# Two chained feed-forward networks in fp32 on one core: the operands of the next pair of blocks formed over six steps with their sums kept in DRAM, the tail's weights loaded two steps ahead, the last results turned on TensorE

## The chip, the cores and the metric

The kernel runs on one core of a Trainium2 chip. The metric is the device time of one execution in microseconds (us). The engines of the core are named as the profile names them: PE (TensorE, matmul; PEld is its weight load), DVE (VectorE), ACT (ScalarE), POOL (GpSimd) and SP (SyncE, which here only issues DMAs; SPq is its queue of instructions). Each engine works through its own list in order and waits at an instruction until what that instruction needs is there.

## The reference

`x` is (8, 8, 512, 64), `state` is (8, 8, 32, 64), everything is fp32. Attention between each head's tokens and its 32 states gives 4608 rows of width 512 (512 token rows and 32 state rows of 8 batches, 8·544 = 4352 output rows in all); two feed-forward networks follow. Cut to what matters here:

```python
def _moe_ref(x, w_gate, w_val, w_out):          # d_ff = 1536
    g = x @ w_gate
    silu = g * (1.0 / (1.0 + np.exp(-g)))
    return silu * (x @ w_val) @ w_out

def _moe2_ref(x, w_in, w_out, alpha):           # d_ff = 2048, the part that is changed
    h = x @ w_in
    g = np.maximum(h, 0.0) + alpha * np.minimum(h, 0.0)
    return g @ w_out
```

## The kernel before

Every fp32 matrix product is made from three products of a high and a low part (`PASSES`, L19): an operand is split into `hi`, a rounded copy written by ACT (L77, `acopy`), and `lo`, the rest, a subtraction on DVE (L83, `sub_lo`). Attention and the first network take the first 741 us; their output goes to DRAM in `x2d`, one tile for each block of 512 tokens. The change is in the second network, which has 8 such blocks in four pairs, and then the state rows.

**A pair and its steps.** The second network works on a pair of blocks with a scheme that needs 7 products where a 2x2x2 multiplication needs 8. For it the input of a pair is wanted in seven *forms* of 128x1024 (`FORMS`: b00, t2, t1, t3, b10, t4, b11), each with hi and lo. Three of them are input blocks; four (t1 to t4) are differences, t1 = b01 − b00, t2 = b11 − t1, t3 = b11 − b01, t4 = b10 − t2. A pair has 8 *steps* s = 0..7, each for 256 of the 2048 hidden columns, so 32 steps t in all; 8 steps for the states follow (the tail, `hidden_last`, L1006 to L1022, `held`, L991).

**A step.** `hidden_pair` (L841) makes 7 products, one for each form, in the order of `FORMS`; a product is a *group* of 6 matmuls of 128x512 (L851) into the PSUM tiles g, v or aux. DVE adds parts together (`plus`, L859), ACT and POOL apply the second network's activation (`raised`, L817 to L823), POOL forms differences (`less`, L863), and the results are split into `h`. After each of the products comes a *place*: `fill()` (L1059) is called, places 1 to 7 of a step. It takes one item from `work`: a *link*, which is the multiplication with `w_out` (`project`, L944), again a group of 6 matmuls (L954) into `acc`, after which DVE adds `acc` into a tile `sum` (L965). Two steps (a *group of steps*) have 7 links for each of two halves e, 14 items; `work` starts with 16 empty items, which sets by how many places the links run behind the products. A step is therefore 14 groups of 6 matmuls on PE.

**Forming the next pair.** At s = 6 `x2_pair` puts 12 actions into the list `nxt`: four loads of raw input tiles x2r from DRAM, four subtractions of 128x1024 (L786), and seven `put`s (L771), each a hi on ACT and right behind it the lo on DVE. `FORMING` (L1048) says at which places one is taken: (s=6, places 1 and 7), all seven of s = 7, and places 1, 2 and 4 of the next pair's s = 0.

**Giving the results.** When a result tile of a pair is complete, it is queued in `giving`. `give` (L969) adds on DVE (L982), turns the 128x512 tile in 32x32 blocks on DVE (L986) and writes it with four DMAs of 64 KB in rows of 128 bytes (L989). One is taken at each third place, when `nxt` is empty; in the tail, at each place. There are eight to a pair.

**Order.** For the 32 pair steps DVE, ACT and POOL run in the order in which the code is written. The lists of PE and SP are set by a scheduler. SP issues all DMAs from one list: the weights `w2` of the products (L758), the weights `wo2` of the links (L941; `load_wo`, three links' at a group's start, then each three links ahead), x2r (L783), the weights of the tail (`load_last`, L762, one step ahead) and the output (L989). When the first of these waits for its data, all behind it wait.

## Time and profile before

| | |
|---|---|
| time, median of 3 runs | 1501.37 us (1499.89 to 1504.82) |
| the profiled execution | 1497.59 us, span 1495.7 us |
| busy: PE / DVE / ACT / POOL | 92% / 70% / 55% / 37% of the span |
| second network, 32 pair steps | 741.4 to 1401.1 us |
| tail (states, last links and results) | 1401.1 to 1495.7 us |
| mean granted PE clock | 0.977 |
| HBM traffic | 195.04 MB read, 58.20 MB written |

The busy shares are averages over two networks with different limits, so the prediction goes by stretches. A step in which PE never waits takes 19.04 us (14 groups of 6 matmuls, 1.36 us each); what a step takes above that is a wait, or slow matmuls after one. In the rows below a timeline row gives start, duration, engine, line, operation, tiles, how many, and in brackets how long the engine stood idle before it and what ended that. A row of grouped instructions ends in busy time, mean ns of one, and idle time before them.

### The profile page before, as it was taken

The numbers are of one execution on the slowest core, as the hardware profiler recorded it, in microseconds if no ns is written. First come the engines' busy times: TensorE is split into PE (matmuls) and PEld (weight loads), VectorE is DVE, ScalarE is ACT, GpSimd is POOL, SyncE is SP. The second block draws the span as 40 slices with busy tenths as digits, with TensorE's granted clock in tenths as the row PEclk, the third lists the DMA queues.
The fourth block names the chain that finished last, engine by engine and source line by source line (L and its number), as shares of the span: only waits on it lengthen the run. The fifth ranks groups of instructions, "written<-read, shape, count | busy, mean of one in ns | idle before, by whom it ended". The sixth has DMA issues, their size and how long they took to land.

```text
span 1495.7 us, 20408 instructions
## 1 busy us (share of the span) xinstructions
PE 1383.1 (92%) x7160; PEld 1066.4 (71%) x7160; DVE 1046.4 (70%) x1599; ACT 819.0 (55%) x1400; POOL 552.4 (37%) x422
## 2 busy tenths in 40 slices
PE   5799999999998999999979988999799998999895
PEld 2466777767676767779958866778577876788784
DVE  6778536677786876345556787887887788778740
ACT  6665344555655545334367655666466655666532
POOL 4432102233231331000065545655454654556511
PEclk7999999999999999999999999999999999999998
DMA  9443150776859565103255656685557756676585
GB/s 265 165 148 63 58 142 2 219 222 195 225 171 271 163 187 140 44 1 127 64 214 174 196 161 185 167 262 183 169 133 226 266 163 190 179 244 222 180 238 183
DMA packets 282142, 254.60 MB, mean 170 GB/s; under 512 B 149944, under 2 KB 210360, under 8 KB 281016
## 3 DMA queue, kind: packets, MB, share of 16 engines
q1 hardware_dynamic: 279896, 252.90, 56.1%
q8 instruction: 57, 0.93, 0.2%
q10 hardware_dynamic: 2144, 0.39, 0.2%
q14 instruction: 45, 0.37, 0.1%
HBM read 195.04 MB, written 58.20 MB: 169 GB/s over the span
## 4 chain that ended last, share of the span: by engine, by line
PE 60%; DVE 17%; ACT 8%; issue 6%; DMA 5%; POOL 2%; SPq 2%; POOLq 0%; DVEq 0%; ACTq 0%
PE acc L502 15%; PE acc L954 11%; PE v L471 9%; PE g L471 8%; PE v L851 5%; DVE h L83 5%; PE g L851 3%; PE aux L851 3%; PE aux L441 3%; DVE u L859 2%; DVE x L83 2%; DVE sum L965 2%; DMA raw<-in_moe_w_out_dram 2%; ACT m L822 1%; ACT m L820 1%
## 5 line engine op out<-in xcount | busy, mean ns | idle before, releaser
L954 PE MATMUL acc<-h,wo 128*128 128x512 f32 x1344 | 352.4, 399 | 28.0 <-DVE sum L965 18.3
L954 PEld LDWEIGHTS acc<-h,wo 128*128 128x128 f32 x1344 | 255.8, 192 | 92.7 <-DVE sum L965 24.9
L502 PE MATMUL acc<-h,wp 128*128 128x512 f32 (+1 forms) x1296 | 296.7, 379 | 7.1 <-DVE h L83 3.7
L502 PEld LDWEIGHTS acc<-h,wp 128*128 128x128 f32 x1296 | 234.0, 189 | 57.6 <-DVE h L83 4.9
L823 POOL TENSOR_TENSOR u<-u,m 128x512 f32<-128x512 f32 x96 | 125.4, 1306 | 363.4 <-ACT m L822 329.8
L83 DVE TENSOR_TENSOR h<-u,h 128x512 fp32r<-128x512 f32 x160 | 155.6, 988 | 59.7 <-ACT h L77 58.9
L851 PE MATMUL v<-x,w 128*128 128x512 f32 x576 | 151.6, 400 | 19.5 <-DVE u L859 19.5
L471 PE MATMUL g<-a,sw 128*128 128x512 f32 x576 | 155.9, 406 | 9.7 <-ACT sw L77 5.4
L471 PEld LDWEIGHTS g<-a,sw 128*128 128x128 f32 x576 | 105.1, 190 | 71.3 <-issue 26.0
L471 PE MATMUL v<-a,sw 128*128 128x512 f32 x576 | 154.4, 404 | 0.2 <-DVE p L487 0.2
L820 ACT ACTIVATE m<-u 128x512 f32<-128x512 f32 x96 | 60.4, 629 | 154.8 <-DVE u L859 154.7
L851 PEld LDWEIGHTS v<-x,w 128*128 128x128 f32 x576 | 108.9, 191 | 47.4 <-DVE u L859 25.0
L965 DVE TENSOR_TENSOR sum<-acc,sum 128x512 f32<-128x512 f32 x184 | 125.2, 682 | 20.3 <-PE acc L954 19.6
L471 PEld LDWEIGHTS v<-a,sw 128*128 128x128 f32 x576 | 107.5, 192 | 34.0 <-issue 10.1
L83 DVE TENSOR_TENSOR h<-h,h 128x512 fp32r<-128x512 f32 (+1 forms) x80 | 81.7, 1021 | 55.4 <-ACT h L77 54.8
L283 POOL TENSOR_TENSOR m<-m,raw 128x512 int32<-128x512 int32 x44 | 61.1, 1393 | 154.0 <-DVE m L275 92.1
L487 DVE TENSOR_TENSOR s<-s,v 128x512 f32<-128x512 f32 (+1 forms) x84 | 54.2, 645 | 83.0 <-PE v L471 68.4
L863 POOL TENSOR_TENSOR u<-u,u 128x512 f32<-128x512 f32 x64 | 106.1, 1658 | 5.0
L77 ACT ACTIVATE h<-u 128x512 fp32r<-128x512 f32 x160 | 96.4, 621 | 18.5 <-POOL u L863 18.5
L83 DVE TENSOR_TENSOR sw<-aux,sw 128x512 fp32r<-128x512 f32 x96 | 62.7, 683 | 56.0 <-ACT sw L77 56.0
L851 PE MATMUL aux<-x,w 128*128 128x512 f32 x384 | 98.9, 391 | 3.0 <-DVE x L83 2.3
L851 PE MATMUL g<-x,w 128*128 128x512 f32 x384 | 98.9, 393 | 2.1 <-ACT h L821 2.1
(143 smaller groups left out, 2091.1 us busy)
## 6 DMA issues: line engine op xcount, KB each, us to landing
wo<-ws2d SPq DMA_DIRECT2D x224, 256.0 KB, 3.9
w<-w2d SPq DMA_DIRECT2D x104, 512.0 KB, 5.2
w2d<-sp SPq DMA_DIRECT2D x32, 512.0 KB, 3.6
raw<-in_moe_w_out_dram SPq DMA_DIRECT2D x14, 1024.0 KB, 5.2
w<-w2d SPq DMA_DIRECT2D x48, 256.0 KB, 4.3
x2d<-xo SPq DMA_DIRECT2D x32, 256.0 KB, 3.5
raw<-in_moe_w_in_dram SPq DMA_DIRECT2D x8, 1024.0 KB, 6.3
wo2d<-sp SPq DMA_DIRECT2D x16, 512.0 KB, 4.1
```

The source lines that it names most:

```text
L77: return nc.scalar.activation(o, i, AF.Copy)
L83: (eng or nc.vector).tensor_tensor(out=o, in0=src, in1=hi.bitcast(F32), op=ALU.subtract)
L283: nc.gpsimd.tensor_tensor(out=m, in0=m, in1=lo, op=ALU.add)
L471: nc.tensor.matmul(o[:, :self.n], self.lhs(f, k, a, which), self.rhs(k, c), start=(i == 0), stop=(i == last))
L487: return nc.vector.tensor_tensor(out=self.p[f], in0=self.p[f], in1=self.product(f, 1, "v"), op=ALU.mult)
L502: nc.tensor.matmul(self.acc[e][:, :self.n], wo1[f // 2][:, f % 2, a, e * P:(e + 1) * P], t[:, c, :self.n], start=(f == 0 and i == 0), stop ...
L820: nc.scalar.activation(n, src, AF.Relu, scale=-1.0)
L823: nc.gpsimd.tensor_tensor(out=out, in0=out, in1=n, op=ALU.add)
L851: nc.tensor.matmul(o, w[:, a, q], x[k][:, q, e], start=start and n == 0, stop=stop and n == 5, skip_group_check=True)
L863: nc.gpsimd.tensor_tensor(out=o, in0=x0, in1=x1, op=ALU.subtract)
L954: nc.tensor.matmul(o, w[:, f, a, e], h[:, q], start=first and i == 0, stop=i == 5, skip_group_check=True)
L965: nc.vector.tensor_tensor(out=r, in0=o, in1=r, op=ALU.add)
```

## The change

- **Sums ahead of time, by way of DRAM.** For pairs 1 to 3 `x2_pair` gives way to two functions. `x2_sums`, registered at s = 1, loads raw tiles at (s=4, place 1), (4, 5) and (5, 4) and makes the four differences at (4, 4), (5, 1), (5, 3) and (5, 7); each is written by SP to `xt2d` in DRAM (512 KB). `x2_forms`, registered at s = 6, loads each form's source again, from `x2d` or `xt2d`, up to five places ahead, makes the hi on ACT at places 4 and 6 of s = 6, 2, 4 and 6 of s = 7, and 1 and 3 of the next s = 0, and the lo on DVE one place later. A transition has 11 loads of 512 KB in place of 4, and 4 writes more.
- **Links one place earlier.** `work` starts with 15 empty items in place of 16.
- **Gives.** The condition for taking one in a pair step is now place number divisible by three and not one of the first four places of s = 0.
- **Last pair's results.** `give_last` makes only the DVE addition; at the next place `turn` makes four PE transposes of 128x128 (L1056 of the new file) into an aux PSUM tile, ACT copies it (no DVE transpose), and one DMA in rows of 512 bytes writes it. In the tail every place takes two items of `work`.
- **Tail weights** are loaded two steps ahead.

```diff
--- before.py
+++ after.py
@@ -94,6 +94,7 @@
     x2d = [dram.tile([P, NPAIR, S if c < B else NS], F32, tag=f"x2d{c}", name=f"x2d{c}")
            for c in range(B + 1)]
     srd = dram.tile([NS, DM], F32, tag="srd", name="srd")
+    xt2d = [dram.tile([P, 4, 2, S], F32, tag=f"xt2d{c}", name=f"xt2d{c}") for c in range(1, B // 2)]
     w2d = [dram.tile([P, 8, 2, 2, P], F32, tag=f"w2d{j}", name=f"w2d{j}") for j in range(NJ2)]
     ws2d = [dram.tile([P, 7, 2, 2, P], F32, tag=f"ws2d{j}", name=f"ws2d{j}") for j in range(NJ2)]
     wo2d = [dram.tile([P, 2, 2, DM], F32, tag=f"wo2d{j}", name=f"wo2d{j}") for j in range(NJ2)]
@@ -774,6 +775,57 @@
             sub_lo(t[:, :, 1, :n], src[:, :, :n], t[:, :, 0, :n])
             return t
 
+        def x2_raw(pr, d, c):
+            t = t4([P, 2, S], F32, "x2r")
+            nc.sync.dma_start(t, x2d[2 * pr + c][:, 2 * d:2 * d + 2, :])
+            return t
+
+        def x2_sums(pr):
+
+            r = {}
+
+            def load(d, c):
+                r[d, c] = x2_raw(pr, d, c)
+
+            def sub(k, x0, x1, to):
+                nc.vector.tensor_tensor(out=r[to], in0=r[x0], in1=r[x1], op=ALU.subtract)
+                nc.sync.dma_start(xt2d[pr - 1][:, k], r[to])
+
+            b00, b01, b10, b11 = [(d, c) for d in range(2) for c in range(2)]
+            return {(4, 1): lambda: (load(*b00), load(*b01)), (4, 4): lambda: sub(0, b01, b00, b00),
+                    (4, 5): lambda: load(*b11), (5, 1): lambda: sub(2, b11, b01, b01),
+                    (5, 3): lambda: sub(1, b11, b00, b11), (5, 4): lambda: load(*b10),
+                    (5, 7): lambda: sub(3, b10, b11, b10)}
+
+        def x2_forms(pr):
+
+
+            x, places = x2.setdefault(pr, {}), {}
+
+            def load(k):
+                if FORMS[k][0] == "b":
+                    x["raw", k] = x2_raw(pr, int(FORMS[k][1]), int(FORMS[k][2]))
+                else:
+                    t = x["raw", k] = t4([P, 2, S], F32, "x2r")
+                    nc.sync.dma_start(t, xt2d[pr - 1][:, int(FORMS[k][1]) - 1])
+
+            def hi(k):
+                x[FORMS[k]] = t8([P, 2, 2, S], F32R, "x2")
+                acopy(x[FORMS[k]][:, :, 0], x["raw", k])
+
+            def lo(k):
+                t = x[FORMS[k]]
+                sub_lo(t[:, :, 1], x.pop(("raw", k)), t[:, :, 0])
+
+            def put(at, th):
+                places.setdefault((NJ2 - 2 + (at - 1) // 7 if at < 15 else 0, (at - 1) % 7 + 1), []).append(th)
+
+            for k, at in enumerate((4, 6, 9, 11, 13, 15, 17)):
+                put(max(1, at - 5), lambda k=k: load(k))
+                put(at, lambda k=k: hi(k))
+                put(at + 1, lambda k=k: lo(k))
+            return places
+
         def x2_pair(pr):
 
             r, x = {}, x2.setdefault(pr, {})
@@ -923,7 +975,7 @@
             for k, o in (("t1", h00), ("t3", h01), ("t2", h11), ("t4", h10)):
                 left[k] = lambda k=k, o=o: (hi(k, o), lo(k, o))
 
-        acc, sums, put_in, giving = {}, {}, set(), []
+        acc, sums, put_in, giving, turning = {}, {}, set(), [], []
 
         def store(u, o):
             nq = P // Ns
@@ -964,7 +1016,10 @@
             else:
                 nc.vector.tensor_tensor(out=r, in0=o, in1=r, op=ALU.add)
             if s == NJ2 - 2 and k in ("h10", "t2", "t3", "t4"):
-                giving.append(lambda: give(pr, to, e))
+                if pr < B // 2 - 1:
+                    giving.append(lambda: give(pr, to, e))
+                else:
+                    give_last(pr, to, e)
 
         def give(pr, to, e):
 
@@ -987,6 +1042,23 @@
             for i in range(4):
                 dst = out[c * T:c * T + S, d * P + 32 * i:d * P + 32 * i + 32]
                 nc.sync.dma_start(dst.rearrange("(t r) n -> r t n", r=32), o[32 * i:32 * i + 32])
+
+        def give_last(pr, to, e):
+
+            d, c = 2 * e + int(to[1]), 2 * pr + int(to[2])
+            r = sums[pr, to][:, e]
+            if to != "o00":
+                nc.vector.tensor_tensor(out=r, in0=sums[pr, "p1"][:, e], in1=r, op=ALU.add)
+
+            def turn():
+                pt = aux([P, SC, P])
+                for k in range(SC):
+                    nc.tensor.transpose(pt[:, k, :], r[:, k * P:(k + 1) * P], ident)
+                o = t2([P, SC, P], F32, "o")
+                acopy(o, pt)
+                nc.sync.dma_start(out[c * T:c * T + S, d * P:(d + 1) * P].rearrange("(k p) n -> p k n", k=SC), o)
+
+            turning.append(turn)
 
         def held(t, u):
 
@@ -1044,27 +1116,28 @@
         blk.finish(B)
 
         LAST = (B // 2) * NJ2
-
-        FORMING = {(NJ2 - 2, 1): 1, (NJ2 - 2, 7): 1, (0, 1): 1, (0, 2): 1, (0, 4): 1}
-        FORMING.update({(NJ2 - 1, i): 1 for i in range(1, 8)})
-
         def step(t, pr, s):
-            if t >= LAST - 1 and t + 1 < len(STEPS):
-                load_last(t + 1)
+            for n in ((t + 1,) if t == LAST - 1 else (t + 1, t + 2) if t == LAST else (t + 2,) if t > LAST else ()):
+                if n < len(STEPS):
+                    load_last(n)
+            if s == 1 and pr + 1 < B // 2:
+                forming.update(x2_sums(pr + 1))
             if s == NJ2 - 2 and pr + 1 < B // 2:
-                nxt.extend(x2_pair(pr + 1))
+                forming.update(x2_forms(pr + 1))
             n = 7 if t < LAST else 2
             places = [0]
 
             def fill():
                 places[0] += 1
-                for _ in range(1 if t < LAST else 4 if len(work) > 6 else 2):
+                for _ in range(len(turning)):
+                    turning.pop(0)()
+                for _ in range(1 if t < LAST else 2):
                     if work:
                         work.pop(0)()
-                for _ in range(FORMING.get((s, places[0]), 0) if t < LAST else 0):
-                    if nxt:
-                        nxt.pop(0)()
-                if giving and (t >= LAST or (t * n + places[0]) % 3 == 0 and not nxt):
+                ths = forming.pop((s, places[0]), ()) if t < LAST else ()
+                for th in ths if isinstance(ths, (list, tuple)) else [ths]:
+                    th()
+                if giving and (t * n + places[0]) % 3 == 0 and (s or places[0] > 4):
                     giving.pop(0)()
 
             if pr == B // 2 - 1 and s == NJ2 - 2:
@@ -1082,7 +1155,7 @@
                     load_wo(t // 2, n)
                 work.extend(lambda n=n, e=e, link=link: link(n, e) for n in range(len(LINKS)) for e in range(2))
 
-        nxt, work = [], [lambda: None for _ in range(2 * 7 + 2)]
+        forming, work = {}, [lambda: None for _ in range(2 * 7 + 1)]
         with tc.manual_schedule(engines={mybir.EngineType.DVE, mybir.EngineType.Activation, mybir.EngineType.Pool}):
             for t in range(LAST):
                 step(t, *STEPS[t])
@@ -1090,7 +1163,7 @@
                 th()
         for t in range(LAST, len(STEPS)):
             step(t, *STEPS[t])
-        for th in giving + work:
+        for th in turning + work:
             th()
 
 
```

The order on **DVE** around s = 7 of pair 0, where pair 1's operands are formed. `x2r` are raw tiles, `x2t` a difference, `x2` a form, `h2` the split hidden values, `u`, `v`, `p1` and `aux` parts of the products, `sum` and `acc` a link's result. Before, from the first subtraction on:

```order
L786 TENSOR_TENSOR x2t_1429_7979<-x2r_1402_7825,x2r_1401_7823 128x1024
L83 TENSOR_TENSOR h2_1425_7961<-h_1417_7912,h2_1425_7961 128x512
L965 TENSOR_TENSOR sum_1310_7287<-acc3_1433_7994,sum_1310_7287 128x512
L83 TENSOR_TENSOR x2_1434_8002<-x2r_1401_7823,x2_1434_8002 128x2x512
L859 TENSOR_TENSOR u_1436_8012<-v_1435_8005,p1_1432_7991 128x512
L83 TENSOR_TENSOR h2_1425_7961<-u_1420_7934,h2_1425_7961 128x512
L965 TENSOR_TENSOR sum_1318_7333<-acc2_1428_7971,sum_1318_7333 128x512
L786 TENSOR_TENSOR x2r_1401_7823<-x2r_1404_7829,x2t_1429_7979 128x1024
L83 TENSOR_TENSOR h2_1421_7936<-h_1417_7912,h2_1421_7936 128x512
L965 TENSOR_TENSOR sum_1318_7333<-acc3_1433_7994,sum_1318_7333 128x512
L83 TENSOR_TENSOR x2_1440_8048<-x2r_1401_7823,x2_1440_8048 128x2x512
```

After, the same part of the program, from the first lo on:

```order
L83 TENSOR_TENSOR x2_1419_7925<-x2r_1405_7849,x2_1419_7925 128x2x512
L911 TENSOR_TENSOR u_1424_7961<-v_1407_7853,p1_1404_7839 128x512
L83 TENSOR_TENSOR h2_1425_7963<-u_1416_7908,h2_1425_7963 128x512
L1017 TENSOR_TENSOR sum_1306_7273<-acc2_1428_7974,sum_1306_7273 128x512
L911 TENSOR_TENSOR u_1432_7994<-aux_1411_7880,u_1408_7860 128x512
L1017 TENSOR_TENSOR sum_1306_7273<-acc3_1435_8003,sum_1306_7273 128x512
L83 TENSOR_TENSOR x2_1429_7982<-x2r_1406_7851,x2_1429_7982 128x2x512
L83 TENSOR_TENSOR h2_1433_7996<-h_1422_7941,h2_1433_7996 128x512
L1017 TENSOR_TENSOR sum_1316_7322<-acc2_1428_7974,sum_1316_7322 128x512
L911 TENSOR_TENSOR u_1442_8044<-v_1441_8037,p1_1438_8022 128x512
L83 TENSOR_TENSOR h2_1433_7996<-u_1424_7961,h2_1433_7996 128x512
```

Before, two subtractions of 128x1024 and two lo stand in 11 rows; after, two lo and no subtraction: the four (L791 of the new file) stand 45, 34, 28 and 15 rows ahead of the first lo.

The order on **SP** at the end of step 17 and the start of step 18 (s = 2 of pair 2): `out_dram` are the four DMAs of a give, `wo2` the links' weights, two loads to a link, `w2` the products' weights. Before and after:

```order
L758 DMA w2_1775_9972<-w2d2_99 128x1024
L989 DMA out_0_dram<-o_1779_9991 32x16x32 x4
L941 DMA wo2_1780_9998<-ws2d0_105 128x512
L941 DMA wo2_1780_9998<-ws2d1_106 128x512
L941 DMA wo2_1781_10001<-ws2d0_105 128x512
L941 DMA wo2_1781_10001<-ws2d1_106 128x512
```

```order
L1044 DMA out_0_dram<-o_1779_9955 32x16x32 x4
L993 DMA wo2_1792_10042<-ws2d0_108 128x512
L1044 DMA out_0_dram<-o_1791_10035 32x16x32 x4
L993 DMA wo2_1792_10042<-ws2d1_109 128x512
L993 DMA wo2_1793_10045<-ws2d0_108 128x512
L993 DMA wo2_1793_10045<-ws2d1_109 128x512
```

One of the first link's two loads has moved ahead of the give, the other still stands behind it. On **PE** the first link of that group of steps (`wo2_1780` before, `wo2_1792` after) stood behind the third product of step 18 (aux) and now stands behind the second (v):

```order
L851 MATMUL g_1783_10007<-x2_1691_9465,w2_1760_9874 128x512 x6
L954 MATMUL acc2_1765_9901<-h2_1704_9545,wo2_1758_9855 128x512 x6
L851 MATMUL v_1786_10026<-x2_1697_9511,w2_1760_9874 128x512 x6
L954 MATMUL acc3_1771_9935<-h2_1704_9545,wo2_1758_9855 128x512 x6
L851 MATMUL aux_1788_10049<-x2_1703_9540,w2_1768_9927 128x512 x6
L954 MATMUL acc0_1791_10061<-h2_1747_9796,wo2_1780_9998 128x512 x3
L954 MATMUL acc0_1791_10061<-h2_1777_9976,wo2_1780_9998 128x512 x3
```

```order
L903 MATMUL g_1795_10051<-x2_1682_9405,w2_1772_9918 128x512 x6
L1006 MATMUL acc3_1778_9946<-h2_1717_9592,wo2_1767_9872 128x512 x6
L903 MATMUL v_1798_10070<-x2_1692_9462,w2_1772_9918 128x512 x6
L1006 MATMUL acc0_1801_10087<-h2_1761_9844,wo2_1792_10042 128x512 x3
L1006 MATMUL acc0_1801_10087<-h2_1789_10020,wo2_1792_10042 128x512 x3
L903 MATMUL aux_1803_10098<-x2_1706_9538,w2_1781_9972 128x512 x6
L1006 MATMUL acc1_1805_10107<-h2_1761_9844,wo2_1792_10042 128x512 x3
```

In the **tail on PE**, from one product of the states (L1015 before, L1087 after) to the next of the links; before, and then after with the transposes of one give (`aux_2253`):

```order
L1015 MATMUL g_2233_12670<-x2_2154_12175,w2_2213_12539 128x256 x6
L1015 MATMUL g_2233_12670<-x2_2156_12180,w2_2213_12539 128x256 x6
L954 MATMUL acc0_2228_12642<-h2_2176_12307,wo2_2219_12581 128x512 x3
L954 MATMUL acc0_2228_12642<-h2_2204_12476,wo2_2219_12581 128x512 x3
```

```order
L1087 MATMUL g_2249_12698<-x2_2172_12236,w2_2231_12600 128x256 x6
L1087 MATMUL g_2249_12698<-x2_2174_12241,w2_2231_12600 128x256 x6
L1056 MATMUL aux_2253_12720<-ident_77,sum_2066_11612 128x128 x4
L1006 MATMUL acc3_2245_12674<-h2_2200_12397,wo2_2228_12578 128x512 x3
L1006 MATMUL acc3_2245_12674<-h2_2225_12560,wo2_2228_12578 128x512 x3
```

What moved: four transposes stand between the states' product and the links that follow it, eight times in the tail.

## Rows read from the trace of the kernel before

**Rows 1.** Windows: single steps, the three transitions, one dense stretch.

```profile
core 0: us, PE busy (x) PEld busy (x) DVE busy (x) ACT busy (x) POOL busy (x), PEclk, DMA share, GB/s
846.40:865.44 19.04, 19.04 (x85) 15.77 (x84) 14.89 (x19) 11.18 (x21) 10.80 (x8) 1.00 0.61 203
865.44:918.89 53.45, 42.44 (x169) 32.05 (x168) 42.51 (x48) 27.93 (x45) 24.73 (x16) 0.97 0.55 175
1038.83:1092.59 53.76, 43.41 (x169) 33.08 (x168) 42.99 (x48) 27.95 (x45) 24.74 (x16) 0.94 0.56 175
1211.46:1264.94 53.48, 44.99 (x169) 34.10 (x168) 42.59 (x48) 27.93 (x46) 24.75 (x16) 0.90 0.54 171
1153.13:1173.38 20.25, 19.36 (x85) 15.69 (x84) 15.46 (x21) 13.51 (x24) 11.35 (x8) 1.00 0.86 280
1173.38:1192.42 19.04, 19.04 (x85) 15.77 (x84) 15.79 (x21) 12.54 (x23) 11.53 (x9) 1.00 0.63 217
1092.59:1111.97 19.38, 19.33 (x86) 15.69 (x84) 17.49 (x25) 12.34 (x22) 11.42 (x8) 1.00 0.44 95
993.00:1001.00 8.00, 8.00 (x37) 6.60 (x37) 5.72 (x9) 7.32 (x14) 3.05 (x3) 1.00 1.02 382
```

**Rows 2.** Waits of PE from 738 us on; DMA issues of the page.

```profile
PE v L851 <- DVE u L859: 19.5, 13, 2.4
PE acc L954 <- DVE sum L965: 18.3, 14, 5.2
PE g L1015 <- DMA w<-w2d: 5.6, 3, 4.0
...
wo<-ws2d SPq DMA_DIRECT2D x224, 256.0 KB, 3.9
```

**Rows 3.** Groups of DVE instructions in the first transition (865.4 to 919).

```profile
L83 DVE TENSOR_TENSOR x<-x2r,x 128x1024 fp32r<-128x1024 f32 x6 | 9.3, 1552 | 6.4 <-ACT x L77 6.4
...
L786 DVE TENSOR_TENSOR x2r<-x2r,x2r 128x1024 f32<-128x1024 f32 x2 | 3.8, 1889 | 0.0
L786 DVE TENSOR_TENSOR x2t<-x2r,x2r 128x1024 f32<-128x1024 f32 x1 | 1.8, 1840 | 2.0 <-PE acc L954 2.0
...
L786 DVE TENSOR_TENSOR x2r<-x2r,x2t 128x1024 f32<-128x1024 f32 x1 | 1.7, 1711 | 0.0
L83 DVE TENSOR_TENSOR x<-x2t,x 128x1024 fp32r<-128x1024 f32 x1 | 1.5, 1474 | 2.3 <-ACT x L77 2.3
```

**Rows 4.** Timeline of DVE in that transition: two subtractions of one shape.

```profile
870.13 0.68 DVE L83 TENSOR_TENSOR h<-h,h 128x512 fp32r<-128x512 f32 x1
...
877.18 1.78 DVE L83 TENSOR_TENSOR h<-h,h 128x512 fp32r<-128x512 f32 x1
```

**Rows 5.** Timelines of DVE, SP and PE at the start of step 18.

```profile
1114.93 0.71 DVE L986 STREAM_TRANSPOSE o<-sum 128x512 f32<-128x512 f32 x1
...
1115.67 1.95 SPq L989 DMA_DIRECT2D out_dram<-o  x4
1117.71 2.82 SPq L941 DMA_DIRECT2D wo<-ws2d  x6
...
1120.62 1.55 PE L954 MATMUL acc<-h,wo 128*128 128x512 f32 x4 [1.67 <-DMA wo<-ws2d]
```

**Rows 6.** The same of PE in step 12, SP and PE in step 20.

```profile
989.10 0.93 PE L954 MATMUL acc<-h,wo 128*128 128x512 f32 x3 [1.22 <-DMA wo<-ws2d]
...
1155.78 3.46 SPq L941 DMA_DIRECT2D wo<-ws2d  x5
...
1161.14 1.52 PE L954 MATMUL acc<-h,wo 128*128 128x512 f32 x6
```

**Rows 7.** Timeline of PE: a long wait in the tail; four transposes elsewhere.

```profile
1414.81 2.50 PE L954 MATMUL acc<-h,wo 128*128 128x512 f32 x5 [5.24 <-DVE sum L965]
...
646.45 0.65 PE L653 MATMUL aux<-ident,xsn 128*128 128x128 f32 x4
648.33 1.98 PE L502 MATMUL acc<-h,wp 128*128 128x512 f32 x8
```

## The prediction

> **What bounds the kernel now.** I read the windows by step first. A step in which PE never waits lasts 19.04 us, and in it DVE is busy for 14.89 (the first row of [rows 1]). The three transitions, s = 7 of a pair with s = 0 of the next, last 53.45, 53.76 and 53.48 us where two free steps take 38.08. That is 15.37 + 15.68 + 15.40 = 46.45 us over the floor, the largest loss in the second network that has one place. Next, the list of PE's waits: it waits longest for DVE, 19.5 us for the parts of the products and 18.3 us for the link additions [rows 2]. Then DVE's groups in the first transition: forming the operands takes 9.3 + 1.5 us for seven lo and 3.8 + 1.8 + 1.7 us for four subtractions, 18.1 in all, and DVE stands idle 6.4 + 2.3 us because a lo follows directly behind the hi that ACT must first write, and 2.0 us ahead of the first subtraction [rows 3]. Busy 42.51 plus these 10.7 us idle make 53.2 of 53.45 us: DVE sets the pace of the whole transition, by work that comes in a lump and by waits for ACT. In the other steps it has some 4 us to spare.
>
> **Part one: the forming.** The work on DVE stays (four subtractions, seven lo) but is spread, and its idle time should go, since each lo stands one place, 2.72 us, behind its hi. A mean subtraction takes 7.3/4 = 1.83 us, a mean lo 10.8/7 = 1.54. Without the forming the first transition holds 42.51 − 18.1 = 24.4 us of DVE work, 12.2 to a step; the step before it holds 14.89. I take the middle, 13.6, for s = 7 and s = 0. For s = 4 and 5 I take the rows of pair 2, 15.46 and 15.79 [rows 1].
>
> After the change DVE has in s = 4 one subtraction, 15.5 + 1.8 = 17.3; in s = 5 three, 15.8 + 5.5 = 21.3; in s = 6 two lo, 14.9 + 3.1 = 18.0; in s = 7 three, 13.6 + 4.6 = 18.2; in the next s = 0 two, 13.6 + 3.1 = 16.7. Together 91.5 of 95.2 us, so it fits, but s = 5 is over by 2.3, and the steps around it have little to give back. A step with DVE at 17.49 us lasted 19.38, 0.34 above the floor [rows 1]; I take 0.3 for each of s = 4, 6 and 7. That leaves 2.3 + 0.9 = 3.2 us in a transition, 9.6 in three, and the gain is 46.45 − 9.6 = **36.9 us**. The ends: nothing is left, a gain of 46.5; or each of the 11 operations still puts PE back by one short DVE instruction (0.68 us, [rows 4]), 7.5 a transition and 22.4 in all, a gain of 24. A gain larger than 46.5 is excluded by the floor.
>
> What the rows show of a mutual hindrance: two DVE subtractions of one shape in this transition took 0.68 and 1.78 us [rows 4]. The Trainium skill (SBUF — State Buffer, "SBUF: two separate sides") says that DVE with two SBUF inputs and GpSimd hold one port pair exclusively and the other one fully blocks. That speaks against this change: POOL is busy for 24.73 of 53.45 us in the transition (0.46) but for 0.56 to 0.61 of s = 4 and 5 [rows 1], so forming operations that move there would meet it more often: 11 operations × 0.11 (the rise of the share) × 1.1 us (1.78 − 0.68) = 1.3 us a transition, 4 us in all, and the sum below would be −24 in place of −28.
>
> The DMA side. A transition moves 15 tiles of 512 KB in place of 4. Spread over five steps, 15 × 0.524 MB / 95 us is 83 GB/s. The fullest step measured, s = 4 of pair 2, ran at 280 GB/s and a DMA share of 0.86; a dense stretch of 8 us reached 382 GB/s with PE at work throughout [rows 1]. 280 + 83 = 363 fits, barely, so I cost it at nothing. The loads stand up to five places, 13.6 us, ahead of use. SP waits at each of the four writes for the subtraction, and the weights of the products and links queue behind it. The cover is that these are issued some steps' places ahead; if it is gone, the price is the third rival's.
>
> **Part two: the links one place earlier.** One place is two groups of 6 matmuls, 2.72 us. PE's total work is the same, but the first link of a group of steps needs its weights 2.72 us sooner, and where a give stands ahead of those loads in SP's list, they can't be issued sooner. Step 18 shows the chain: DVE's transpose at 1114.93 runs 0.71 us, SP issues the four output DMAs from 1115.67, the weights only from 1117.71, and PE starts the link at 1120.62 after 1.67 us of waiting [rows 5]. Step 12 shows the same with 1.22 us [rows 6]. The gives' places hardly change, so both waits grow by up to 2.72 us, less some 0.4 where one of the two loads has moved ahead of the give: 2.4 each, 4.8 together. In step 20 the weights were issued from 1155.78; with the median landing of 3.9 us [rows 2] they came at 1159.7, and the link ran at 1161.14 [rows 6], so 1.4 us of slack turns into a wait of 1.3. For one more start of this kind in pair 3 I take 2. Sum **+8 us**. The ends are +4 (only the two starts that wait already) and +12 (four full places, 10.9, and slow matmuls behind them).
>
> **Part three: the tail.** Loading the states' weights two steps ahead, and writing each result by one DMA instead of four, should remove the three waits for `w2d`, **−5.6** [rows 2]. The longest wait, 5.24 us for DVE's addition of a link [rows 7], has another cause and stays. The turning costs PE 32 transposes. In the first network four of the same shape with 6 matmuls took 648.33 − 646.45 = 1.88 us, 0.52 above the 1.36 of the matmuls [rows 7]; eight times is **+4.2**. Each turn waits for an addition that DVE has just been given; for three of the eight I take 0.7, **+2**. DVE loses eight transposes, but it isn't the bound in the tail. Sum **+1**, between −6 (only the removed waits count) and +6 (weights that come no sooner). The Trainium skill (TensorE: Matmul & The Clock Gate, Part 4: PE-mode transpose) gives about 275 ns for a 128x128 transpose in bf16; by that figure the 32 would take 8.8 us, and the tail would be +5 instead of +1.
>
> **The sum.** −36.9 + 8 + 1 = −28 us. The profiled execution took 1497.59 us, so 1469.6 for a like one; it lay 3.8 us below the median of 1501.37, so **1473 us** against that median. All low ends together give −48.5, all high ends −6: 1453 to 1495.
>
> **The rivals.**
> 1. *The lump only gets flatter.* If s = 7 and s = 0 need 14.9 us like a steady step, the five steps hold 94.1 of 95.2 us, 99%, and any irregularity comes back as a wait. If half of the 46.5 us stays, the sum is −23.2 + 8 + 1 = −14, **1487**. For it speaks that DVE's work is the same, and that s = 5 is over its floor; against it the 10.7 idle us in a transition that need not be there.
> 2. *Everything hides.* PE's waits at the group starts give DVE time in s = 4, and nothing is left: −46.5 + 4 − 1 = −43.5, **1458**. Against it: s = 5 at 21.3 us.
> 3. *The weights starve* (slower). SP's list holds four more waiting writes and 11 loads, the links want their weights 2.72 us sooner, and every one of the 12 group starts of pairs 1 to 3 waits as steps 12 and 18 do, about 1.2 + 2.7 = 3.9 us: +47, in all −36.9 + 47 + 1 = +11, **1512**. It decides the sign from 36/12 = 3 us a start. For it: a DMA share of 0.86 already in s = 4. Against: of the 12 starts only two wait now, and the others lie further behind a give.
> 4. *Nothing on balance.* The first part ends at 24, the second at 12, the third at 6: −6, **1495**; the lump has become small waits everywhere.
>
> **How the numbers follow.** Forecast 0.55 (its own range 1464 to 1482), rival 1 0.20, rival 2 0.12, rival 3 0.06, rival 4 0.07. A measurement of this kernel tells about 0.3%, 4.5 us, from no change. The forecast and rivals 1 and 2 are faster by more (0.87), rival 4 lies at the bound and is counted as no change (0.07), rival 3 is slower (0.06). The range takes in the forecast with its unknown costs and rivals 1 and 2, each at its own time, and leaves out the far ends of the bounds with rivals 3 and 4: 1457 to 1492.
>
> **What would show it.** Right: the three transitions last 40 to 43 us each, no DVE idle time for ACT ahead of a lo, s = 5 is the longest of the five steps with DVE over 95%, the links at the start of steps 12 and 18 wait about 4 us for their weights, the waits for `w2d` in the tail are gone and each turn adds about half a microsecond. Wrong: s = 4 to s = 6 each over 21 us (rival 1), waits of PE for `w2` or `wo2` at most group starts with SP standing at a write to `xt2d` (rival 3), or forms that arrive late from DRAM, which I cost at nothing.

## The result and the profile after

The changed kernel takes 1481.64 us (median of 4 runs, 1478.91 to 1488.22) against 1502.36 of the kernel before beside it: a ratio of 0.9869, 95% interval 0.9832 to 0.9906, so 21 us or 1.3% faster. The forecast was −28 us; the time lies in the stated range. The profiled execution has a span of 1477.1 us against 1495.7.

Three stretches of the two traces add up to the difference. The 32 pair steps take 645.80 us (659.64 before), the tail 89.0 (94.6 before), and all that comes earlier 742.3 (741.4; no edit touches it, and it varied from 739.6 to 748.1 in the runs below). −13.8 − 5.6 + 0.9 = −18.5. Because of that variation the runs below are compared by pair steps and tail, not by span.

Windows of the changed kernel, columns as in [rows 1]: the 32 pair steps, the three transitions, then s = 7 and s = 5 of pair 0, steps 12 and 18, and the tail.

```profile
core 0: us, PE busy (x) PEld busy (x) DVE busy (x) ACT busy (x) POOL busy (x), PEclk, DMA share, GB/s
742.31:1388.11 645.80, 608.41 (x2601) 490.34 (x2599) 504.81 (x624) 404.60 (x698) 368.46 (x250) 0.99 0.71 228
867.64:909.74 42.10, 39.34 (x170) 31.21 (x169) 36.89 (x44) 28.60 (x46) 24.95 (x17) 1.00 0.77 252
1035.83:1077.91 42.08, 39.29 (x170) 31.21 (x168) 36.84 (x44) 28.59 (x46) 24.91 (x17) 1.00 0.76 251
1204.22:1246.34 42.12, 39.33 (x169) 31.23 (x168) 36.90 (x44) 28.60 (x46) 24.96 (x17) 1.00 0.77 248
867.64:889.99 22.35, 19.98 (x85) 15.52 (x84) 18.07 (x22) 14.30 (x23) 12.44 (x9) 1.00 0.81 266
828.24:848.60 20.36, 19.33 (x86) 15.69 (x84) 17.74 (x21) 10.76 (x20) 12.73 (x8) 1.00 0.94 321
972.77:996.70 23.93, 21.21 (x85) 16.78 (x84) 15.38 (x20) 12.64 (x23) 12.21 (x9) 0.93 0.88 290
1097.76:1122.43 24.67, 20.91 (x86) 16.86 (x84) 14.53 (x20) 13.79 (x26) 10.61 (x8) 0.93 0.70 214
1388.11:1477.10 88.99, 71.57 (x411) 61.99 (x409) 28.56 (x46) 32.47 (x82) 20.63 (x22) 0.94 0.60 211
```

The transitions, 53.5 to 53.8 us in [rows 1], are 42.1 each. Against that, step 12 has become 23.93 us long (20.51 before) and step 18 24.67 (21.39 before). PE's waits from 738 us on, to be held against [rows 2] and one more line of the kernel before, which stands first:

```profile
PE acc L954 <- DMA wo<-ws2d: 2.9, 2, 1.7
```

```profile
PE acc L1006 <- DVE sum L1017: 19.0, 19, 6.1
PE acc L1006 <- DMA wo<-ws2d: 11.6, 5, 3.8
PE v L903 <- DVE u L911: 5.0, 5, 2.1
```

The wait for the parts of the products is 5.0 us where it was 19.5, that for `w2d` is gone, the waits for link additions are about as before, and the wait for the links' weights has grown from 2.9 to 11.6 us. DVE's groups of forming work follow, the lo of the kernel before first; the idle time ahead of them (the last numbers) was 20.1 + 7.0 us there ([rows 3] shows 8.7 of that) and is 1.1 now:

```profile
L83 DVE TENSOR_TENSOR x<-x2r,x 128x1024 fp32r<-128x1024 f32 (+1 forms) x20 | 31.0, 1555 | 20.1 <-ACT x L77 20.1
...
L83 DVE TENSOR_TENSOR x<-x2t,x 128x1024 fp32r<-128x1024 f32 x3 | 4.4, 1473 | 7.0 <-ACT x L77 7.0
```

```profile
L83 DVE TENSOR_TENSOR x<-x2r,x 128x1024 fp32r<-128x1024 f32 (+1 forms) x23 | 33.2, 1446 | 1.1 <-ACT x L77 0.9
L791 DVE TENSOR_TENSOR x2r<-x2r,x2r 128x1024 f32<-128x1024 f32 x12 | 20.6, 1720 | 0.0
```

### The profile page after: what moved, and what is told of

Same layout as the page of the kernel before. It is cut to its first block, busy times and chain, and to the rows that moved or that the text cites. A ratio compares the mean times of both kernels' runs of the same rounds, so it can differ in the third digit from the quotient of the medians.

```text
span 1477.1 us, 20530 instructions
## 1 busy us (share of the span) xinstructions
PE 1379.3 (93%) x7192; PEld 1067.1 (72%) x7192; DVE 1033.7 (70%) x1591; ACT 822.6 (56%) x1408; POOL 558.8 (38%) x422
## 4 chain that ended last, share of the span: by engine, by line
PE 57%; DVE 16%; ACT 10%; issue 6%; DMA 5%; POOL 4%; SPq 2%; POOLq 0%; ACTq 0%; DVEq 0%
PE acc L503 16%; PE v L472 9%; PE g L472 9%; PE acc L1006 8%; DVE h L83 6%; PE v L903 3%; PE aux L442 3%; DVE u L911 3%; PE g L903 2%; PE aux L903 2%; DMA wo<-ws2d 2%; ACT h L77 2%; DVE sum L1017 2%; ACT m L874 2%; DMA raw<-in_moe_w_out_dram 2%
## 5 line engine op out<-in xcount | busy, mean ns | idle before, releaser
L1006 PEld LDWEIGHTS acc<-h,wo 128*128 128x128 f32 x1344 | 251.5, 190 | 101.2 <-DVE sum L1017 28.1
L875 POOL TENSOR_TENSOR u<-u,m 128x512 f32<-128x512 f32 x96 | 128.5, 1338 | 354.3 <-ACT m L874 322.7
L83 DVE TENSOR_TENSOR h<-u,h 128x512 fp32r<-128x512 f32 x160 | 159.0, 1009 | 69.4 <-ACT h L77 68.4
L83 DVE TENSOR_TENSOR h<-h,h 128x512 fp32r<-128x512 f32 (+1 forms) x80 | 77.7, 972 | 62.5 <-ACT h L77 62.0
L915 POOL TENSOR_TENSOR u<-u,u 128x512 f32<-128x512 f32 x64 | 103.1, 1611 | 5.0
L77 ACT ACTIVATE h<-s 128x512 fp32r<-128x512 f32 (+1 forms) x84 | 50.3, 598 | 89.9 <-DVE s L488 89.7
```

The source lines that it names most:

```text
L77: return nc.scalar.activation(o, i, AF.Copy)
L83: (eng or nc.vector).tensor_tensor(out=o, in0=src, in1=hi.bitcast(F32), op=ALU.subtract)
L875: nc.gpsimd.tensor_tensor(out=out, in0=out, in1=n, op=ALU.add)
L915: nc.gpsimd.tensor_tensor(out=o, in0=x0, in1=x1, op=ALU.subtract)
L1006: nc.tensor.matmul(o, w[:, f, a, e], h[:, q], start=first and i == 0, stop=i == 5, skip_group_check=True)
```

## The experiments

Each run is read by its stages, all in us. "Lag" is the number of empty items that `work` starts with, "s = 7" and "s = 5" are those steps of pairs 0, 1, 2, and "wo" is PE's wait for the links' weights. A row is one profiled execution; only the changed kernel, e9 and e10 were timed four times. How far single rows can be trusted shows where kernels share code: pair steps that differ in nothing but the last pair's results came out at 645.8, 645.8 and 646.7 (changed, e3, e11), and at 659.6 and 659.5 (before, e8). Tails differ more: e7 and e10 have the tail code of the changed kernel and its lag, and theirs lasted 91.2 and 91.0 us where it had 89.0.

| kernel | pair steps | tail | s = 7 | s = 5 | wo |
|---|---|---|---|---|---|
| before | 659.6 | 94.6 | 24.95, 26.47, 24.97 | 19.04 each | 2.9 |
| changed | 645.8 | 89.0 | 22.35, 22.31, 22.33 | 20.36, 20.06, 20.05 | 11.6 |
| e1 changed, lag 16 | 634.6 | 88.4 | 22.34, 22.35, 22.36 | 20.49, 23.10, 21.15 | 3.2 |
| e2 before, lag 15 | 673.8 | 96.8 | 22.94, 22.79, 23.38 | 19.04 each | 14.5 |
| e3 changed, old tail | 645.8 | 96.1 | as changed | as changed | 13.7 |
| e4 before, hi earlier | 645.6 | 95.7 | 24.42, 24.70, 24.43 | 19.04 each | 3.6 |
| e5 = e1, forms at idle places | 629.1 | 88.4 | 19.34, 21.46, 21.41 | 20.49, 23.33, 21.19 | 1.8 |
| e6 = e5, two and two subtractions | 616.5 | 88.4 | 19.04 each | 19.04, 20.84, 19.77 | 3.3 |
| e7 changed, wo asked for early | 630.5 | 91.2 | 22.36, 22.31, 22.33 | 20.35, 20.19, 20.92 | none |
| e8 before, tail weights two ahead | 659.5 | 89.9 | as before | as before | 3.0 |
| e9 = e6 with wo early, lag 16 | 612.1 | 89.5 | 19.04 each | 19.04, 20.09, 19.15 | none |
| e10 = e9 with lag 15 | 610.3 | 91.0 | 19.04 each | 19.04, 19.04, 19.11 | none |
| e11 changed, old gives | 646.7 | 92.3 | as changed | as changed | 12.9 |

### The lag of the links, undone and done alone

```diff
@@ e1, from the changed kernel
-        forming, work = {}, [lambda: None for _ in range(2 * 7 + 1)]
+        forming, work = {}, [lambda: None for _ in range(2 * 7 + 2)]
@@ e2, from the kernel before
-        nxt, work = [], [lambda: None for _ in range(2 * 7 + 2)]
+        nxt, work = [], [lambda: None for _ in range(2 * 7 + 1)]
```

> The changed kernel with 16 empty items at the start of work, so the links run as far behind the products as before; all else as changed. Theory (the links one place earlier wait for weights that SP can't issue ahead of a give): the waits for wo of 11.6 us at PE fall to about 3, the steps (1,3), (1,4), (2,2), (2,4), (3,4) lose 3 to 5 us each, and the span falls by 14 to 17 us from 1477.1 to about 1461. Rival (these waits come from the added transfers through DRAM, whatever the lag): the span stays within 4 us of 1477 and the waits for wo stay at 8 us or more.

> The kernel before with 15 empty items in place of 16, nothing else. Theory (the lag alone costs 14 to 17 us): the span rises from 1495.7 to about 1510, with waits for wo of some 11 us. Rival (it costs only beside the added transfers): within 4 us of 1495.7, waits for wo at 3 to 6 us.

The span of e1 is 1466.2 us, its pair steps are 11.2 us shorter than the changed kernel's; the wait for the weights falls from 11.6 to 3.2. That is less than the 14 to 17 expected. The five steps named did fall by 17.0 us together, but s = 5 of pairs 1 and 2 grew from 20.06 and 20.05 to 23.10 and 21.15, and step 10 by 1.5. My reading is that while PE waited just ahead of s = 5, DVE caught up, and that without the wait its backlog reaches s = 5. No run isolates this: in e7 below the waits for weights are gone as well, and there s = 5 of pair 2 grows to 20.92, but that of pair 1 stays at 20.19. In e2 the lag alone adds 14.2 us to the pair steps of the kernel before and 2.3 to the tail, with no transfer through DRAM beside it. The waits of e2:

```profile
PE acc L954 <- DMA wo<-ws2d: 14.5, 4, 4.6
```

So the rival, that the added transfers make the links wait, falls. One place less of lag, with the weights asked for where they were, is a loss in either kernel.

### Where the links' weights stand in SP's list

```diff
@@ fill(), from the changed kernel
+                if t < LAST and t % 2 and places[0] == 4:
+                    for m in range(3):
+                        load_wo(t // 2, m)
@@ the end of step()
-                for n in range(3):
-                    load_wo(t // 2, n)
```

> The changed kernel (15 empty items) in which the first three links' weights of a group of steps are asked for at place 4 of the odd step instead of at its end, three places earlier in SP's order, ahead of the gives there; nothing else. Theory (the links one place earlier lose time because SP stands at a give ahead of their weights): the waits for wo fall from 11.6 to under 3 us, the steps (1,4), (2,2), (2,4), (3,4) from 23.9, 24.7, 22.9, 24.0 to 19 to 21, the pair steps from 645.8 to about 632 to 636. Rival (the links lose time on something else that is late, hidden values or sums): the waits for wo fall, but those four steps stay above 22 us with other waits in their place.

The waits for wo are gone, steps 12, 18, 20 and 28 last 19.04, 19.39, 20.25 and 19.06 us, and the pair steps fall by 15.3 to 630.5, a little more than expected. The rival falls: nothing else was late at these places. Step 11 is another matter. It stays at 23.47 us (23.69 in the changed kernel, 20.69 in e1), because its link waits not for weights but for a copy on ACT, 2.73 us in the changed kernel and 1.32 in e1:

```profile
953.33 2.59 PE L1006 MATMUL acc<-h,wo 128*128 128x512 f32 x6 [2.73 <-ACT sum L77]
```

The chain in the changed kernel (SP, PE and DVE at the start of step 18), to be read against [rows 5]:

```profile
1100.62 0.71 DVE L1041 STREAM_TRANSPOSE o<-sum 128x512 f32<-128x512 f32 x1
```

```profile
1101.36 1.94 SPq L1044 DMA_DIRECT2D out_dram<-o  x4
1103.35 2.41 SPq L993 DMA_DIRECT2D wo<-ws2d  x5
```

```profile
1106.43 0.93 PE L1006 MATMUL acc<-h,wo 128*128 128x512 f32 x3 [3.75 <-DMA wo<-ws2d]
```

Counted from the start of step 18 (1097.76, before 1111.97), DVE's transpose begins 2.86 us in (2.96 before), the weights are issued from 5.59 (5.74), and the link starts 8.67 us in (8.65). The link was asked for earlier and started when it always had: it waits 3.75 us where it waited 1.67. In e7 SP issues the same weights ahead of the give and of step 18's start at 1095.28:

```profile
1083.49 2.81 SPq L993 DMA_DIRECT2D wo<-ws2d  x6
1090.54 1.97 SPq L1044 DMA_DIRECT2D out_dram<-o  x4
```

So the loss of the smaller lag came by way of the weights' place in SP's list. That 630.5 lies 4.1 us under e1's 634.6 does not make 15 empty items better than 16, since e1 still asks for its weights late and waits 3.2 us for them. The fair pair is e9 and e10 further down, both with the weights early: 612.1 and 610.3 us of pair steps, 89.5 and 91.0 of tail, which is no difference that can be told.

### What holds the transitions

> The kernel before in which only ACT's hi of each operand form is made one action of the list earlier than DVE's lo, at the same places for all DVE work; no sums ahead of time, no DRAM. Theory (a transition of 53.5 us is 42.5 us of DVE work and 10.7 of DVE idle, so DVE paces it): the idle time before the lo, 8.7 us in the first transition, nearly goes and each transition shortens by 6 to 9 us to about 45 to 47, span about 1472 to 1477. Rival (only spreading over more steps helps; DVE finds other waits): each transition shortens by less than 3 us.

e4 splits each `put` of the kernel before into hi and lo and moves only the hi:

```diff
...
-                    lambda: put("b00", (0, 0)),
-                    lambda: sub(r[0, 0], r[1, 1], r["t1"]),
-                    lambda: put("t2", (0, 0)), lambda: put("t1", "t1"),
+                    both(first, lambda: hi("b00", s00)),
+                    lambda: lo("b00", s00),
+                    both(lambda: sub(r[0, 0], r[1, 1], r["t1"]), lambda: hi("t2", s00)),
+                    both(lambda: lo("t2", s00), lambda: hi("t1", t1)), lambda: lo("t1", t1),
 ...
```

The transitions last 47.7, 48.0 and 47.7 us, 5.8 less than before (just under the 6 to 9 expected, well over the rival's 3), and DVE's idle time ahead of the lo is 0.9 us in place of 20.1 + 7.0:

```profile
L83 DVE TENSOR_TENSOR x<-x2r,x 128x1024 fp32r<-128x1024 f32 (+1 forms) x20 | 28.8, 1442 | 0.9 <-ACT x L77 0.9
...
L83 DVE TENSOR_TENSOR x<-x2t,x 128x1024 fp32r<-128x1024 f32 x3 | 3.6, 1215 | 0.0
```

So of the 34 us that the changed kernel takes from the three transitions (160.7 to 126.3) half, 17 us, can be had by the hi one place earlier, without a byte through DRAM; spreading the work gives the other half. (The rest of e4's pair steps grew by 3.2 us.)

What keeps s = 7 of the changed kernel at 22.35 us is not a lack of DVE time: it is busy for 18.07 of them in the window above (the expectation of e5 has 19.3, which is too much). Timelines of DVE, ACT, DVE again and PE there:

```profile
878.35 1.72 DVE L83 TENSOR_TENSOR x<-x2r,x 128x1024 fp32r<-128x1024 f32 x1
879.99 1.77 DVE L83 TENSOR_TENSOR h<-u,h 128x512 fp32r<-128x512 f32 x1
881.68 0.68 DVE L911 TENSOR_TENSOR u<-v,p 128x512 f32<-128x512 f32 x1
```

```profile
883.12 0.63 ACT L872 ACTIVATE m<-u 128x512 f32<-128x512 f32 x1 [5.17 <-DVE u L911]
...
884.94 1.05 ACT L77 ACTIVATE x<-x2r 128x1024 fp32r<-128x1024 f32 x1
```

```profile
886.53 1.29 DVE L83 TENSOR_TENSOR h<-u,h 128x512 fp32r<-128x512 f32 x2 [2.85 <-ACT h L77]
887.74 0.68 DVE L1017 TENSOR_TENSOR sum<-acc,sum 128x512 f32<-128x512 f32 x1
```

```profile
888.48 1.67 PE L1006 MATMUL acc<-h,wo 128*128 128x512 f32 x6 [1.66 <-DVE sum L1017]
```

The lo at 878.35 and an h at 879.99 run ahead of the addition for the product v, which so comes at 881.68. ACT has stood idle 5.17 us for it, DVE then stands idle 2.85 us for ACT's next hi, the link's addition behind that hi comes late, and PE waits 1.66 us for it. So a lo just ahead of that addition puts back a chain over two engines. In the undisturbed step of the kernel before DVE has its idle time behind that addition (made at 856.42), time that a lo there can fill:

```profile
860.32 1.97 DVE L83 TENSOR_TENSOR h<-u,h 128x512 fp32r<-128x512 f32 x2 [1.90 <-ACT h L77]
```

e5 moves the places, e6 also the subtractions:

```diff
@@ e5, from e1
-            for k, at in enumerate((4, 6, 9, 11, 13, 15, 17)):
+            for k, at in enumerate((3, 6, 7, 10, 13, 14, 17)):
@@ e6, from e5
-            return {(4, 1): lambda: (load(*b00), load(*b01)), (4, 4): lambda: sub(0, b01, b00, b00),
-                    (4, 5): lambda: load(*b11), (5, 1): lambda: sub(2, b11, b01, b01),
-                    (5, 3): lambda: sub(1, b11, b00, b11), (5, 4): lambda: load(*b10),
-                    (5, 7): lambda: sub(3, b10, b11, b10)}
+            return {(3, 4): lambda: (load(*b00), load(*b01)),
+                    (4, 1): lambda: (sub(0, b01, b00, b00), load(*b11)),
+                    (4, 4): lambda: sub(2, b11, b01, b01), (4, 5): lambda: load(*b10),
+                    (5, 1): lambda: sub(1, b11, b00, b11),
+                    (5, 4): lambda: sub(3, b10, b11, b10)}
```

> The kernel of the run with 16 empty items (pair steps 634.6 us, each s = 7 22.35 us), in which only the places of the operand forms change: the hi at places 3 and 6 of s = 6, 7 (as its first), 3, 6, 7 and the next 3, counted on from s = 6 as 3, 6, 7, 10, 13, 14, 17, each lo one place later, so that a lo stands at places 1, 4 and 7, where DVE stood idle 1.28 and 1.90 us in the undisturbed step from 846.40 of the kernel before, and no longer at 3 and 5, ahead of the additions of v. Theory (s = 7 is over its floor not for a lack of DVE time, 19.3 us of 22.35, but because a lo ahead of an addition of v puts back a chain over ACT and POOL): s = 7 falls from 22.35 to 19.0 to 20.5 us, some 6 to 10 us in the three. Rival (DVE's sum of work decides): s = 7 with s = 0 stay at 42.1 us within 1.

> The same with the subtractions moved too: two in s = 4 (places 1 and 4) and two in s = 5 (1 and 4) in place of one and three; the raw loads one to four places earlier. Theory (s = 5 is over by 1.45, 4.06 and 2.11 us with 16 empty items because three subtractions put DVE at 19 to 22 us): s = 5 falls to 19.0 to 19.8, s = 4 rises by less than 1, another 4 to 6 us in all. Rival (the excess goes where the subtraction goes): s = 4 and s = 5 together stay within 1.5 us.

In e5 s = 7 of pair 0 falls from 22.34 to 19.34 us, as the theory has it; in pairs 1 and 2 only to 21.4, and these are the pairs whose s = 5 overran by 4.3 and 2.2. The three together lost 4.8 us, below the 6 to 10 expected, and s = 0 another 2.2. In e6, with two and two subtractions (in e1 DVE was busy for 18.0, 20.4 and 18.8 us in the three s = 5, somewhat less than the 19 to 22 expected), all three s = 7 and all three s = 0 last 19.04 us, the floor, s = 5 falls by 5.4 us over the three (that of pair 1 only to 20.84, short of the 19.8 expected), s = 4 grows by 1.0, and the pair steps lose 12.6 us. That is more than expected, because s = 7 of pairs 1 and 2 falls too: the backlog of s = 5 had still held it. So the order decides s = 7 only where the sum of DVE's work leaves no backlog from the steps before. s = 7 of pair 0 in e5 and in e6:

```profile
865.73:885.06 19.33, 19.33 (x85) 15.69 (x84) 17.62 (x23) 13.86 (x23) 12.21 (x8) 1.00 0.76 266
```

```profile
869.70:888.74 19.04, 19.04 (x86) 15.77 (x85) 17.55 (x22) 13.55 (x23) 12.07 (x8) 1.00 0.77 268
```

### The tail, in parts

e3 gives the changed kernel the whole tail of before (the gives, one step ahead, four items at a place); e11 only the old gives; e8 gives the kernel before only the loads two steps ahead:

```diff
@@ e8, from the kernel before; e3 has its inverse, and the old gives and places, in the changed kernel
-            if t >= LAST - 1 and t + 1 < len(STEPS):
-                load_last(t + 1)
+            for n in ((t + 1,) if t == LAST - 1 else (t + 1, t + 2) if t == LAST else (t + 2,) if t > LAST else ()):
+                if n < len(STEPS):
+                    load_last(n)
@@ e11, from the changed kernel
-                if pr < B // 2 - 1:
-                    giving.append(lambda: give(pr, to, e))
-                else:
-                    give_last(pr, to, e)
+                giving.append(lambda: give(pr, to, e))
...
-                if giving and (t * n + places[0]) % 3 == 0 and (s or places[0] > 4):
+                if giving and (t >= LAST or (t * n + places[0]) % 3 == 0 and (s or places[0] > 4)):
...
```

> The changed kernel with the tail of before: gives of the last pair turned on DVE with four DMAs each, tail weights one step ahead, four items of work at a place while more than six are left. Theory (the tail part is worth the 5.6 us that the two tails differ by): the tail lasts 94 to 95 us where the changed kernel has 89.0, the 32 pair steps stay at 645.8 us, span about 1482.5. Rival (what I predicted, the tail part is worth nothing and the shorter tail comes from the earlier links): the tail stays at 89 to 90.

> The kernel before in which only the states' weights are loaded two steps ahead, with the old gives and four items of work at a place. Theory A (the three waits for w2d, 5.6 us, come from loads that are asked for too late): they go, and the tail falls from 94.6 to 87 to 89.5. Theory B (they come from SP standing at the 32 output DMAs and their additions; the one DMA for each result is what helped): the tail stays above 92.

> The changed kernel with the last pair's results turned on DVE and written by four DMAs each as before; the states' weights stay two steps ahead and two items of work at a place. Prediction (turning on TensorE costs PE 4.2 us and 2 us of waits): the tail is some 5 us shorter than the changed kernel's 89.0, about 83 to 85. Rival (PE gets the 4.7 us of the transposes back, in shorter waits for DVE and faster matmuls behind them): the tail is 89 to 92. The 32 pair steps stay at 645.8 us, but for the first results of the last pair.

e3: 96.1 us, 7.1 more than the changed kernel, so the tail part is worth more than the two tails differ by; the earlier links cost the tail something (in e1, with the same tail code as the changed kernel, its first link waits 3.8 us for DVE in place of 6.1). e8: 89.9 us (0.4 over the range expected), so the loads alone take 4.7; the wait for `w2d` falls from 5.6 to 0.3, theory A holds. e11: 92.3 us. So turning on TensorE, with one DMA to a result, makes the tail *shorter*, where my prediction had the turning cost 6 us. How much shorter is less sure than 92.3 against 89.0 looks: against the tails of e7 and e10, which are of the same code as the changed kernel's, it is 1.1 and 1.4 us. The waits of e11's tail, with the one for `w2d` that the changed kernel has not, the windows of the tails of e11, e7 and e10 (PEclk 0.90, 0.91 and 0.91 where the changed kernel has 0.94), and the transposes of the changed kernel:

```profile
PE acc L1006 <- DVE sum L1017: 6.1, 1, 6.1
PE g L1084 <- DMA w<-w2d: 3.4, 3, 1.4
```

```profile
1389.37:1481.70 92.33, 72.09 (x379) 61.72 (x377) 33.08 (x54) 28.51 (x74) 20.57 (x22) 0.90 0.68 204
```

```profile
1375.31:1466.53 91.22, 73.35 (x411) 63.23 (x409) 28.38 (x45) 32.29 (x82) 20.51 (x22) 0.91 0.59 206
```

```profile
1349.91:1440.87 90.96, 73.32 (x411) 63.23 (x409) 28.33 (x45) 32.25 (x82) 20.49 (x22) 0.91 0.59 206
```

```profile
L1056 PE MATMUL aux<-ident,sum 128*128 128x128 f32 x32 | 4.7, 274 | 0.5 <-ACT h L873 0.4 <-DVE sum L1051 0.2
```

The transposes keep PE busy for 4.7 us, near the 4.2 predicted, and it waits 0.5 us for them. What pays for that is only in part located. In e11 the loads of the states' weights stand behind eight output DMAs at a time, and PE waits 3.4 us for them. But the 32 output DMAs alone do not make that wait: e8 has them too, with the loads two steps ahead, and waits 0.3. At a lag of 16 PE's first link in the tail waits 3.8 us for DVE in e1 where e8 has 5.2. The granted clock differs as well: 0.91 to 0.95 in the seven tails with transposes, 0.89 to 0.91 in the six without. What sets it, no run separates; and no run separates the turning on PE from the single DMA to a result.

### All that helped, together

e9 is e6 with the weights asked for early, e10 the same with 15 empty items.

> All that helped, together: 16 empty items, the forms at the places where DVE stood idle, two and two subtractions, and the links' first weights of a group of steps asked for at place 4. The run with 16 empty items and these forms had 616.5 us of pair steps, 88.4 of tail, and 3.3 us of waits for wo with slow matmuls behind them in step 18 (22.97 us). Theory (the parts add up, since each removes a wait at a place of its own): pair steps 611 to 614 us, tail 88 to 90, span 1442 to 1450, some 3.5% below the kernel before. Rival (with the weights early, DVE loses the time that PE's waits in s = 4 gave it): s = 5 rises by what s = 4 loses, pair steps stay at 615 to 618.

> The same with 15 empty items, so the links run one place earlier as in the changed kernel. Theory (the lag costs only by the weights that stand behind a give in SP's list; with these asked for early, 630.5 against 634.6 us of pair steps spoke for 15): pair steps within 3 us of the run with 16, tail 1 to 3 us longer because its first link waits longer for DVE. Rival (the places of the lo fit only a lag of 16, since the links' additions and ACT's copies shift by a place against them): pair steps 5 us or more longer than with 16.

Medians of four: e9 takes 1449.47 us, a ratio of 0.9645 to the kernel before (interval 0.9609 to 0.9681), e10 1445.69 us, 0.9632 (0.9595 to 0.9669). Both beat the kernel before by some 3.6%, and the changed kernel, by the two ratios to the kernel before, by some 2.3%; between them no difference can be told. In e9 the pair steps (612.1), the tail and the span came out inside the ranges expected, so the parts add up, and in e10 the places of the lo fit the other lag too. A step of e10 in which PE never waits has DVE at work for 17.5 to 18.2 of 19.04 us:

```profile
863.60:882.64 19.04, 19.04 (x85) 15.77 (x84) 17.54 (x22) 13.57 (x23) 12.05 (x8) 1.00 0.86 283
962.33:981.37 19.04, 19.04 (x86) 15.77 (x84) 18.20 (x21) 11.72 (x22) 14.29 (x8) 1.00 0.92 282
```

## Why the prediction was right, and in which terms it was wrong

The sign and the likeliest mechanism were right, and the range of 1457 to 1492 holds 1481.6. The terms of the sum were not: −36.9 + 8 + 1 was forecast; the runs make it −25.1 + 11.8 − 6.2. The first two came out 11.8 and 3.8 us worse than forecast and the third 7.2 better, so part of the closeness of the total, −19.5 against −28, is luck: with the tail as forecast the gain would have been some 12 us.

- **The forming: −25.1 in place of −36.9** (pair steps of e1 against the kernel before). That DVE paces the transitions with 42.5 us of work and 10.7 of idle time was right, and so were the end of that idle time and, in total, the term of s = 5: I took 2.3 us a transition, 7 in all, and e1 shows 1.5, 4.1 and 2.1, 7.6 in all (the changed kernel itself 3.4). The step that failed is the 0.3 us for s = 7. It was read from the *sum* of DVE's work in a step; the measured excess is 3.3 us in each, 10 in all, and s = 0 has 0.7 where I took nothing. In the sum 18.2 us fit into 19.04 (18.07 were measured); in the order they stood ahead of an addition that ACT waits for. e5 (pair 0) and e6 (all three) show that three lo in s = 7 at other places cost nothing. The −25.1 also holds the new condition for the gives, which no run takes out by itself.
- **The links one place earlier: +11.2 and 0.6 in the tail, in place of +8.** The mechanism, the give ahead of the weights in SP's list, was the predicted one, as e7 shows. The size was off: steps 12, 18, 20 and 28 grew by 3.4, 3.3, 2.7 and 5.0 us, 14.4 in all. The single wait of step 18 grew by 2.1 as worked out (2.4), but the clock fell behind it, 0.93 in the windows of steps 12 and 18, and step 28, for which I took 2 without a row, has 5.0. Step 11 grew by another 3.0, with its wait for ACT's copy, which the forecast did not have at all. Part of this came back elsewhere, 3.0 and 1.1 us of it in s = 5 of pairs 1 and 2 if one goes by e1.
- **The tail: −6.2 at a lag of 16 in place of +1.** The 5.6 us of waits for `w2d` went, as predicted (4.7 of them by the loads alone, e8), and the transposes kept PE busy for what the row of four others said. The step that failed is to add that time, and 2 us of waits, to the tail in full. At a lag of 16 what is left beside the loads comes out at −1.5 (e1 against e8; −0.4 by the tail of e9) in place of +6.2. Where it is given back is open for the most part, as said above.
- **Costed at nothing:** the way through DRAM. In s = 5 the DMA share is 0.94 at 321 GB/s, under the 363 feared, and PE waits for no form.
- **The Trainium skill** (SBUF — State Buffer, "SBUF: two separate sides") would have made the forming operations dearer where POOL is busier, by some 4 us by my estimate. The rows speak against that estimate here: the 12 subtractions take 1720 ns each, against 1867 in the kernel before (11.4 + 5.9 + 5.1 us in 12), and the lo 1446 against 1552 in [rows 3]. On the transposes, the 275 ns that the Trainium skill gives for one (TensorE: Matmul & The Clock Gate, Part 4: PE-mode transpose; there in bf16) are what one of them lasts here, 274; but 32 of them kept PE busy for 4.7 us, 147 ns each: they overlap. Worked out from that figure the 32 were priced too high.
- **The rivals.** The first (half of the lump stays, 1487) lies 5 us above the measured time, nearer than the forecast 9 us below it, but by another mechanism: not the sum of DVE's work but ill-placed operations. The third (weights starve) was right in kind at four of the twelve starts, and too small to turn the sign. Of the signs named, the transitions of 40 to 43 us, the lo without idle time ahead and the vanished waits for `w2d` came true, and the links of steps 12 and 18 waited 2.72 and 3.75 us (about 4 named). "s = 5 is the longest of the five steps with DVE over 95%" was wrong: DVE is busy for 17.74 of its 20.36 us, and s = 7 is the longest, but for s = 4 with its wait for weights.

## What to carry to other kernels

Work that is spread to fill an engine's idle time has to be placed by the order, and not by the sum alone: ask for each place which instruction stands next on that engine and who waits for it, and put the filler behind what starts a chain over other engines (19.04 us against 22.35 here with the same three lo). When consumers are moved earlier, move the loads that feed them as well, past whatever in the same queue waits for an engine. And keep the time that work takes on an engine apart from what it adds to the end: here 4.7 us of transposes on PE did not make the tail longer, and where the time came from was only partly found.

## What the runs showed of the hardware

DVE busy for 18.20 of 19.04 us (96%) and a DMA share of 0.92 went together with a PE that never waited (e10, the window from 962.33), where [rows 1] had shown a step with 17.49 us of DVE work already above the floor. A wait of PE of 2.7 to 3.8 us cost more than itself where the granted clock fell behind it: steps 12 and 18 of the changed kernel show a mean of 0.93 and are 4.9 and 5.6 us over the 19.04 for 2.72 and 3.75 us of waiting. Two stretches behind the first of these waits show the lower of the clock's two levels (0.50, 1.2 GHz) and then the upper (1.00, 2.4 GHz) again:

```profile
981.20:984.40 3.20, 3.20 (x9) 2.46 (x9) 1.29 (x2) 0.00 (x0) 1.28 (x2) 0.50 1.00 344
984.60:996.00 11.40, 11.40 (x51) 9.39 (x50) 9.14 (x13) 6.48 (x12) 2.59 (x2) 1.00 0.94 332
```

It does not fall behind every such wait: step 11 of e10 waits 2.78 us, keeps a clock of 1.00 and is 3.2 us over.
